# Gating the next loads on q^T, and issuing q^T about a quarter of a unit earlier, in a fused attention and feed-forward kernel

## The chip, the cores and the metric

The kernel runs on one core of one Trainium2 chip. The metric is the device time of one execution in microseconds (us), lower is better. A "span" is the time from the first to the last instruction of the one execution that was profiled, which is 1 to 2 us shorter than its run time.

## The reference

Eight batches of linear attention (Linformer), each with 8 heads, 1024 rows and 64 columns a head; then a feed-forward block on the 8192 x 512 result.

```python
k_proj = np.einsum('ks,bhsd->bhkd', E, k)          # 1024 rows -> 64
v_proj = np.einsum('ks,bhsd->bhkd', F, v)
scores = scale * np.matmul(q, k_proj.transpose(0, 1, 3, 2))
attn = softmax(scores)                             # cut: max, exp, sum
x = np.matmul(attn, v_proj)                        # -> [8192, 512]
h1, h2 = x @ w1, x @ w2
out = np.maximum(h1, h2) @ w_out
```

## The kernel before

All instructions are laid out by hand. The feed-forward block is cut into sixteen units, two for each batch; a unit has down products (`P`, line 636) and, between them, the up products of the next unit (`U`, line 558) in two halves of seven, numbered from 0. The attention of batch b is worked in small steps put into these slots. `("G", n, h)` stands before the up products of half h in unit n; `("U", n, h, i)` after up product i of that half. From batch 3 on one batch needs, in this order:

```python
    for b in range(3, B):
        t = tiles[b]
        n = 2 * b - 3
        at_slot(("G", n, 0), new_attn, t)
        at_slot(("G", n, 0), step_qt_dma, t, 0, H // 2)        # q^T, heads 0-3
        at_slot(("G", n, 0), step_qt_dma, t, H // 2, H)        # q^T, heads 4-7
        at_slot(("U", n, 0, 1), step_kv, t, 0, H, "kv", True, True)  # k, v projected; k turned
        at_slot(("U", n, 0, 6), step_gate, t)                  # waits for the turned k
        at_slot(("U", n, 0, 6), loads, b + 1, "k", "v", "q")   # the next batch's loads
```

The two kinds of transposing DMAs are issued by SyncE, in order with the stores of the output (in batch 4 q^T at 138.16 us, a store at 144.43, the turn of k at 145.46). The gate is a copy of one element on GpSimd; the loads stand behind it in GpSimd's program and were issued after it (in batch 4 the copy ran at 148.30 us, and the k load was issued at 148.81):

```python
    def step_kpt_dma(t):                      # "the turn of k": 512 pieces of 256 bytes
        nc.sync.dma_start_transpose(
            out=t["kpt"], in_=t["kp"].rearrange("p h r d -> p (h r d)"))

    def step_gate(t, n="kpt"):
        nc.gpsimd.tensor_copy(out=junk, in_=t[n][0:1, H - 1, 0:1])

    def load(t, n, src, b, h0, h1):           # float32 in HBM -> float16 on chip, 1024 pieces of 1 KB
        nc.gpsimd.dma_start(
            out=t[n][:, h0:h1],
            in_=src[b, h0:h1].rearrange("h (p c) d -> p h c d", c=NC))
```

The first reader of the turned k is the score product (`score`, line 266), which stands in TensorE's order at `("G", n, 1)`. Batch 2 is turned on TensorE, has no turn of k by DMA, and its gate is on q^T (`step_gate, t, "qt"`).

The softmax here doesn't subtract the row's maximum and nothing guards it: scores larger than these inputs give would overflow.

## Time and profile before

| | before |
|---|---|
| time, median of 3 (range) | 327.46 us (326.99 to 328.31) |
| span of the profiled run | 327.0 us |
| TensorE busy | 317.0 us (97%) |
| granted TensorE clock, mean | 0.998 |

The prediction shows the busy times, the waits and the timelines of one batch and says how to read them. Two more lines: the first, from the page, is the granted clock of TensorE in 40 slices of the span, in tenths of full speed. The second, from the view of the instructions of line 223 (the turn of k), gives the time from issue to landing of its five DMAs: shortest, median, longest.

```profile
PEclk9999999999999999999999999999999999999999
```

```profile
DMA to landing us min/median/max: 2.7/2.7/4.4
```

There is no slice below 9, and the turn of k lands 2.7 us after its issue, but for batch 6 with 4.4.

### The profile page before, as it was taken

To read this page: it belongs to the slowest core of one execution; us is meant where nothing else is said; L and a number is where in the kernel's file an instruction comes from. 1 tells how busy PE (TensorE), PEld (TensorE's weight loads), DVE (VectorE), ACT (ScalarE), POOL (GpSimd) and SP (SyncE) were. 2 spreads that over 40 slices of the span, in tenths; PEclk is the share of its full clock that TensorE was granted. 3 is DMA by queue.
4 is the path that set the end of the run, shared out by engine and by line. 5 is a ranking of instruction groups with operands and counts; after the bars stand their busy time and mean duration, and the time that the engine had idled before them with its cause. 6 is when DMAs were issued, how large, how long until landed. Compare 5 with 4: busy or idle time off the path is not lost.

```text
span 327.0 us, 9015 instructions
## 1 busy us (share of the span) xinstructions
PE 317.0 (97%) x3856; PEld 248.5 (76%) x3856; DVE 239.6 (73%) x424; ACT 201.2 (62%) x359; POOL 37.1 (11%) x56
## 2 busy tenths in 40 slices
PE   8989999999999999999999999998999999999995
PEld 3554446878887788878887888877887888888884
DVE  1345898895969778777967796975967796969572
ACT  2365321667777677667776777656776777765541
POOL 8556002003000120003000300003000000000000
PEclk9999999999999999999999999999999999999999
DMA  8999999988999899996999599886999221312133
GB/s 155 204 199 174 204 207 208 217 187 159 176 239 228 143 146 235 219 186 95 211 220 181 115 188 242 184 163 89 219 209 221 57 97 34 98 34 96 35 116 111
DMA packets 74680, 53.14 MB, mean 163 GB/s; under 512 B 29456, under 2 KB 74512, under 8 KB 74640
## 3 DMA queue, kind: packets, MB, share of 16 engines
q0 software_dynamic: 29376, 28.31, 54.9%
q1 hardware_dynamic: 45264, 24.25, 30.6%
q8 instruction: 30, 0.49, 0.6%
q14 instruction: 10, 0.08, 0.1%
HBM read 57.15 MB, written 16.78 MB: 226 GB/s over the span
## 4 chain that ended last, share of the span: by engine, by line
PE 78%; DMA 17%; DVE 2%; issue 1%; POOL 1%; ACT 0%; SPq 0%; POOLq 0%; DVEq 0%
PE mm_ps L636 44%; PE mm_ps L558 25%; DMA q_sb<-in_q_dram 8%; DMA v_sb<-in_v_dram 4%; PE att_ps L180 3%; PE att_ps L278 3%; PE mm_ps L266 3%; DMA k_sb<-in_k_dram 2%; DMA big<-in_moe_w_dram 2%; DMA kpt_sb<-kp_sb 1%; DVE gt_sb L573 1%; PE mm_ps L237 1%; DVE o_sb L660 1%; DVE xt_sb L381 0%; POOL v_sb L102 0%
## 5 line engine op out<-in xcount | busy, mean ns | idle before, releaser
L529 ACT COPY p_sb<-mm_ps 128x512 f32<-128x512 f32 x172 | 97.2, 593 | 41.3 <-PE mm_ps L558 30.2
L636 PEld LDWEIGHTS <-big 128*128 128x128 f16 x768 | 73.6, 98 | 12.0 <-issue 3.1
L636 PE MATMUL mm_ps<-T_sb,big 128*128 128x256 f16 x576 | 77.8, 273 | 0.0
L573 DVE TENSOR_TENSOR gt_sb<-mm_ps,p_sb 128x512 f16<-128x512 f32 x56 | 38.5, 688 | 47.2 <-PE mm_ps L558 44.0
L558 PE MATMUL mm_ps<-big,big 128*128 128x256 f16 x336 | 50.4, 273 | 0.0
L558 PEld LDWEIGHTS <-big 128*128 128x128 f16 x448 | 43.8, 98 | 5.2
L636 PE MATMUL mm_ps<-wo_sb,gt_sb 128*128 128x256 f16 x256 | 43.0, 273 | 0.1
L636 PEld LDWEIGHTS <-gt_sb 128*128 128x128 f16 x384 | 35.7, 98 | 9.7 <-issue 5.4
L558 PEld LDWEIGHTS <-wd_sb 128*128 128x128 f16 x336 | 32.9, 98 | 3.8
L355 ACT ACTIVATE ex_sb<-mm_ps 128x512 f16<-128x512 f32 x50 | 27.2, 597 | 10.5 <-PE att_ps L278 7.0
L558 PE MATMUL mm_ps<-xt_sb,wd_sb 128*128 128x256 f16 x224 | 33.6, 273 | 0.0
L381 DVE TENSOR_TENSOR xt_sb<-att_ps,ld_sb 128x1024 f16<-128x1024 f32 x26 | 31.7, 1219 | 0.1
L660 DVE TENSOR_TENSOR o_sb<-mm_ps,p_sb 128x512 f32<-128x512 f32 x32 | 21.9, 685 | 7.5 <-PE mm_ps L636 7.5
L636 PE MATMUL mm_ps<-m_sb,xt_sb 128*128 128x256 f16 x128 | 24.4, 273 | 0.0
L608 ACT ACTIVATE gt_sb<-mm_ps 128x512 f16<-128x512 f32 x28 | 16.8, 600 | 10.3 <-PE mm_ps L558 10.3
L519 DVE TENSOR_TENSOR big<-gt_sb 128x1024 f16<-128x1024 f16 x32 | 21.9, 685 | 0.2
L576 DVE TENSOR_SCALAR gt_sb<-gt_sb 128x512 f16<-128x512 f16 (+1 forms) x56 | 20.3, 363 | 1.9
L636 PE MATMUL mm_ps<-T_sb,gt_sb 128*128 128x256 f16 x128 | 21.5, 273 | 0.0
L636 PE MATMUL mm_ps<-wo_sb,big 128*128 128x256 f16 x128 | 21.5, 273 | 0.0
L636 PEld LDWEIGHTS <-xt_sb 128*128 128x128 f16 x192 | 18.8, 98 | 2.2
L229 POOL COPY junk<-kpt_sb 1x1 f16<-1x1 f16 x5 | 1.0, 209 | 162.5 <-DMA kpt_sb<-kp_sb 162.5
L573 DVE TENSOR_TENSOR gt_sb<-p_sb 128x512 f16<-128x512 f32 x28 | 19.1, 681 | 0.0
(85 smaller groups left out, 427.3 us busy)
## 6 DMA issues: line engine op xcount, KB each, us to landing
out_dram<-o_sb SPq DMA_DIRECT2D x63, 256.0 KB, 2.9
k_sb<-in_k_dram POOLq DMA_DIRECT2D x7, 1024.0 KB, 10.6
v_sb<-in_v_dram POOLq DMA_DIRECT2D x7, 1024.0 KB, 18.1
q_sb<-in_q_dram POOLq DMA_DIRECT2D x7, 1024.0 KB, 22.3
k_sb<-in_k_dram POOLq DMA_DIRECT2D x4, 256.0 KB, 7.0
q_sb<-in_q_dram POOLq DMA_DIRECT2D x4, 256.0 KB, 8.1
v_sb<-in_v_dram POOLq DMA_DIRECT2D x2, 512.0 KB, 12.2
big<-in_moe_w_dram POOLq DMA_DIRECT2D x8, 128.0 KB, 9.9
```

Source lines behind the costliest of these rows:

```text
L180: nc.tensor.matmul(out=kv_ps[r * KP : (r + 1) * KP, 0:n], lhsT=eft[:, i, c, :], rhs=t[w][:, h0:h1, c, :], start=(c == 0), stop=(c == NC - 1),)
L266: nc.tensor.matmul(out=banks[e][pos : pos + Z, h * W : (h + 1) * W], lhsT=t["kpt"][o * D : (o + 1) * D, head, s * Z : (s + 1) * Z], rhs=t[ ...
L355: nc.scalar.activation(out=t["ex", g, j][:, e, :], in_=banks[e], func=ACTF.Exp, scale=scale)
L381: nc.vector.tensor_tensor(out=x_out(t, g, j).rearrange("q z o n -> q o z n"), in0=at_ps.rearrange("q o (z n) -> q o z n", z=2), in1=ld[:, ...
L519: nc.vector.tensor_tensor(out=S(i), in0=x, in1=y, op=op)
L529: copy(out=x, in_=bank)
L558: nc.tensor.matmul(out=bank[:, m * W : (m + 1) * W], lhsT=w_[:, n_, (2 * d + m) * 128 : (2 * d + m + 1) * 128], rhs=a[:, n_, :], start=(n ...
L573: nc.vector.tensor_tensor(out=c_blk(j, c), in0=two(x), in1=two(y), op=ALU.add)
L576: nc.vector.tensor_scalar_max(ap, ap, 0.0)
L608: nc.scalar.activation(out=out, in_=in_, func=ACTF.Relu)
L636: nc.tensor.matmul(out=bank[:, i * CH : (i + 1) * CH], lhsT=a(c)[:, i * 128 : (i + 1) * 128], rhs=w_(c), start=(n is not None and m == (lo ...
L660: nc.vector.tensor_tensor(out=o_sb, in0=two(x), in1=two(y), op=ALU.add)
```

## The change

The intent: from batch 4 on q^T is placed earlier, by eight of the 35 groups of matmuls in a unit, and the next loads need no longer wait for the turn of k, so that they too start earlier. Batch 2 gates on the first half of q^T.

```diff
-    def step_gate(t, n="kpt"):
-        nc.gpsimd.tensor_copy(out=junk, in_=t[n][0:1, H - 1, 0:1])
+    def step_gate(t, h=H - 1):
+        nc.gpsimd.tensor_copy(out=junk, in_=t["qt"][0:1, h, 0:1])
 ...
-    at_slot(("U", 1, 0, 6), step_gate, t, "qt")
+    at_slot(("U", 1, 0, 6), step_gate, t, H // 2 - 1)
 ...
-        at_slot(("G", n, 0), new_attn, t)
-        at_slot(("G", n, 0), step_qt_dma, t, 0, H // 2)
-        at_slot(("G", n, 0), step_qt_dma, t, H // 2, H)
+        key = ("G", n, 0) if b == 3 else ("U", n - 1, 1, 3)
+        at_slot(key, new_attn, t)
+        at_slot(key, step_qt_dma, t, 0, H // 2)
+        at_slot(key, step_qt_dma, t, H // 2, H)
```

## The prediction

> **What bounds it.** I read the page first, then one long stretch by engine, then who waited for whom, then the timelines of SyncE and GpSimd around one batch, and last the landings of single transfers.
>
> ```profile
> span 327.0 us, 9015 instructions
> PE 317.0 (97%) x3856; PEld 248.5 (76%) x3856; DVE 239.6 (73%) x424; ACT 201.2 (62%) x359; POOL 37.1 (11%) x56
> PE   8989999999999999999999999998999999999995
> DMA  8999999988999899996999599886999221312133
> ```
>
> TensorE is busy nearly everywhere; the DMA row is full too, but only up to slice 30, after which the kernel is no faster. The table by stretches for 54 to 310 us, the part the change can reach (columns: length, then busy us of PE, PEld, DVE, ACT, POOL):
>
> ```profile
> 54.00:310.00 256.00, 254.57 (x3255) 211.37 (x3256) 198.97 (x354) 175.36 (x321) 14.37 (x21) 1.00 0.83 160
> ```
>
> TensorE is idle for 256.00 - 254.57 = 1.43 us in 256, at full clock. So no rearrangement of DMAs can gain more than about 1.4 us here (0.4%), while a delay that reaches TensorE is paid in full. The waits of TensorE, its weight loads and SyncE's queue (total us, times, longest) name the one transfer concerned:
>
> ```profile
> PE mm_ps L266 <- DMA kpt_sb<-kp_sb: 1.1, 1, 1.1
> ...
> PEld L266 <- DMA kpt_sb<-kp_sb: 1.9, 2, 1.4
> ...
> SPq L249 <- DMA q_sb<-in_q_dram: 7.3, 2, 5.6
> ```
>
> L266 is the score product, which reads the turned k (kpt); 1.1 us of the 1.43 is one wait for it. Around batch 4, SyncE's queue and then GpSimd:
>
> ```profile
> 138.16 6.17 SPq L249 DMA_TRANSPOSE qt_sb<-q_sb  x2
> 144.43 0.53 SPq L651 DMA_DIRECT2D out_dram<-o_sb  x1
> 145.46 1.20 SPq L223 DMA_TRANSPOSE kpt_sb<-kp_sb  x1
> ```
>
> ```profile
> 148.30 0.18 POOL L229 COPY junk<-kpt_sb 1x1 f16<-1x1 f16 x1 [32.01 <-DMA kpt_sb<-kp_sb]
> 148.81 0.88 POOL L102 DMA_DIRECT2D k_sb<-in_k_dram  x1 [0.34 <-PE mm_ps L636]
> ```
>
> The order is q^T (two halves, landing at 143.89 and 145.62 in the trace), one store, the turn of k (landing 148.18), the gate's copy, and only then the loads. So **kpt travels alone**: the loads wait for it. Its landings leave nearly no slack. By landing and the first score weight load: batch 4, 148.18 against 148.59; batch 5, 184.16 against 184.43; batch 7, 256.87 against 257.24. That is 0.3 to 0.4 us each. In batch 3 (113.01) TensorE waited about 0.2 us (weight load 0.49), in batch 6 (221.67, 4.43 us after issue where the others take 2.7) 1.1 us.
>
> [...] while loads and stores run together about 120 load and 115 store packets start per us. [...] So one blocked transfer on SyncE holds all behind it. The trace shows this in batch 3: kpt's input is ready at 109.36, but SyncE is still issuing q^T and one store, and issues kpt at 110.35. [...] instructions arrive in 16 KiB blocks by DMA. The trace has 30 such packets of about 1 us, and those at 140.23, 178.31 and 249.67 each fall with q^T packets that take 1.2 to 2.0 us instead of 0.025; that at 219.69 falls on the end of batch 6's kpt. [...] the late kpt of batch 6 probably stays.
>
> **The change, part by part.** The order of instructions on TensorE, VectorE and ScalarE is the same in both builds; nothing is added. Two things move.
>
> (1) *q^T earlier, batches 4 to 7.* The fourth up product is eight groups of four matmuls ahead of the old place, 8 x 0.44 = 3.5 us, but SyncE is in order: q^T passes one store, not more. It now stands behind the sixth store (136.52 + 0.37 + the short waits = 136.95 in batch 4) and not the seventh (138.16): 1.2 us earlier, likewise 1.1 in batches 5 to 7. [...] its landing moves about 1 us: 144.6, 180.9, 216.9, 253.1. kpt is not issued earlier for that: VectorE ends its input copy at 145.39, 181.24, 217.09, 254.06, and kpt goes out 0.1 to 0.2 us later already. Gain on the path: about 0.
>
> (2) *The gate.* Batches 3 to 6 load on q^T's second half. The v load takes the buffer of the q just turned and waits for q^T anyway. Gate to first load takes 0.5 us (148.30 to 148.81), so loads go out at about 145.2, 181.5, 217.5 instead of 148.81, 184.80, 222.31: 3.3 to 4.8 us earlier, just where kpt goes out (145.46, 181.40, 217.24). TensorE never waits for these loads after 60 us, so arriving earlier is worth nothing, but **kpt loses its empty channel**. How much? A load's first packets come 1.4 us after issue and are sparse: some 3, 19, 16 and 69 in its first four half microseconds, about 100 when full. So they start at 146.6, 182.9 and 218.9. kpt's 512 packets ran from 1.0 to 2.2 us after issue: 146.45 to 147.7, 182.4 to 183.6, 218.3 to 219.5. It meets only the thin front of the loads: 20 to 50 packets against 512, which I estimate at 0.3 to 0.8 us of delay. Less 0.3 to 0.4 us of slack in batches 4 and 5, nothing less in batch 6: 0.2 + 0.3 + 0.5 = about +1.0 us.
>
> (3) *Batch 2* gates on the first half of q^T, so k of batch 3 loads some 2 us earlier; q of batch 3 lands perhaps 1.5 us earlier. SyncE waits 1.64 us for that q at 102.0, so q^T and kpt of batch 3 go out earlier and the wait of about 0.2 us there ends; its loads start about 110.5, first packets near 111.9, as kpt (then issued about 109.5) has finished. Gain 0.2 to 0.5 us.
>
> Sum: +1.0 - 0.4 = +0.6 us on 327.46, **328.0 us**.
>
> **Rivals.** *A: the loads hit kpt fully.* Stores issued into running loads land 7 to 12 us after issue (119.08 to 126.32; 84.75 to 96.95) instead of 2.2. If q^T lands 1 us earlier than I reckon, the loads' full stream is on kpt, which at one load packet per kpt packet needs 512/120 = 4.3 us instead of 1.2: 3 us late, in three batches some 8 us, about 335 us. For it: transposes stall as a whole[...], as the instruction fetches show. Against: the thin front, the in-order stores. *B: a gain.* If kpt of batch 6 was late through q^T and the store queued ahead of it (q^T landed at 217.87, kpt issued 217.24), the earlier q^T frees it: -1.1 us, with batch 3 about 326. Against: the fetch at 219.69. *C: SyncE blocks.* q^T before the seventh store could hold stores if q were late; but q would land before 170 us in batch 5 (172.77 less 3.6), with q^T at 172.8, and four output buffers give room. Then nothing changes: 327.5.
>
> **Range and chances.** The floor is 327.46 - 1.4 = 326.1; the three times before spread over 1.3 us. The tail is upward, from A. I take 326.5 to 331.5. Faster by 2% would need 6.5 us where 1.4 are idle: 0.01. Slower by 2% needs over 2 us of late kpt in each of three batches: 0.11. Within 2%: 0.88.
>
> **What would show it.** Right: loads of batches 5 to 7 issued 3 to 5 us earlier; q^T 1.1 us earlier; kpt issued where it was, landing 3 to 3.5 us after issue in batches 4 to 6 and 2.7 in 7; TensorE's idle time in 54 to 310 us still 1 to 4 us, its waits at L266 on kpt, up. Wrong: kpt landing 5 us or more after issue (A), or at 2.7 in batches 4 to 6 (B); kpt issued earlier; a new wait of SyncE for q; any wait elsewhere than L266.

## The result, and the profile after

The changed kernel takes **340.86 us** (median of 6, 337.37 to 342.09) against 327.48 us (median of 6, 326.73 to 328.92). The ratio is 1.0384, with a 95% interval of 1.0332 to 1.0437: slower, and outside the predicted range. Ratios here are the mean time of one kernel's runs over that of the other's of the same rounds, so not quite the ratio of the medians quoted. From here on "before" in a ratio is the kernel before, run beside the experiment.

The page of the changed kernel, with the rows for busy time and clock:

```profile
span 340.3 us, 9015 instructions
...
PE 321.0 (94%) x3856; PEld 250.0 (73%) x3856; DVE 239.6 (70%) x424; ACT 201.5 (59%) x359; POOL 37.1 (11%) x56
...
PE   7979999999999999959999699996999999999995
...
PEclk9999999999999999987999989999999999999999
```

Three holes appear in TensorE's row (5, 6, 6), and the clock row, all 9 before, dips after the first two. The same stretch of 54 to 310 us, in which TensorE was busy 254.57 us before, and TensorE's waits (total us, times, longest):

```profile
54.00:310.00 256.00, 245.43 (x3135) 201.41 (x3136) 189.42 (x336) 168.29 (x308) 14.33 (x21) 0.98 0.82 156
```

```profile
PE mm_ps L266 <- DMA kpt_sb<-kp_sb: 10.5, 3, 4.2
```

The three holes are one wait, three times: the score products of batches 4, 5 and 6 for the turned k. **The loss adds up from two terms**: this wait grew from 1.3 us (1.1 in batch 6 and 0.2 in batch 3) to 10.5, which is 9.2 us, and TensorE's busy time, for the same 3856 matmuls, grew from 317.0 to 321.0, which is 4.0 us; together 13.2 of the 13.3 us by which the span grew.

Around batch 4 (SyncE, then GpSimd, then the chain of work that ended last: start, length, what):

```profile
145.38 1.20 SPq L223 DMA_TRANSPOSE kpt_sb<-kp_sb  x1
```

```profile
145.00 0.18 POOL L229 COPY junk<-qt_sb 1x1 f16<-1x1 f16 x1 [30.55 <-DMA qt_sb<-q_sb]
145.51 0.88 POOL L102 DMA_DIRECT2D k_sb<-in_k_dram  x1 [0.34 <-issue]
```

```profile
145.38 7.51 DMA kpt_sb<-kp_sb
152.90 0.04 issue
152.94 0.62 PE mm_ps L266 x14
```

The turn of k goes out at 145.38, 0.08 us before its old time, and the load 0.13 us after it. The turn then lands after 7.51 us. In batches 5 and 6 it is 6.42 and 6.69, in batches 3 and 7 it is 2.69:

```profile
DMA to landing us min/median/max: 2.7/6.4/7.5
```

**What the turn waits for** can be seen in the DMA packets in the trace. This is my count, in us from the issue of the turn; its data are 512 packets of 256 bytes, followed by 32 packets of 4 bytes, called completion packets here, as the landing is recorded 0.33 to 1.09 us after the last of them began; the last column counts load packets of 1 KB that began before the middle one of those 32:

```
                    data packets     completion packets       landed   load packets
                    first   last     first  middle  last               ahead
before,  batch 4     1.17   2.22      2.02    2.09   2.25      2.72        0
changed, batch 4     1.18   2.35      4.95    5.70   7.18      7.51      236
changed, batch 5     1.17   2.31      4.09    5.24   5.86      6.42      210
changed, batch 6     1.18   2.29      3.74    4.43   5.60      6.69      172
```

The data go as fast as before. It is the 32 tiny completion packets that start 1.7 to 5 us late, after 172 to 236 load packets. TensorE's score product starts only behind the landing: in batch 4 the last data packet began at 147.73 us, the landing is at 152.89 and the score product at 152.94.

Two limits of this reading. In batches 5 and 6 the first load packet is recorded only 2.91 and 2.60 us after the issue of the turn, later than the last completion packet begins without a load (2.25), and between the last data packet and it no packet of any kind begins. So what holds the completion at first is not a load packet that the trace shows under way. And a part of batch 6 is not the load's: its last completion packet (5.60; the other 31 by 4.90) began just after an instruction fetch of 16 KB that ended at 5.54.

### The profile page after: what moved, and what is told of

Same layout as the page of the kernel before. It is cut to its first block, busy times and chain, and to the rows that moved or that the text cites. A ratio compares the mean times of both kernels' runs of the same rounds, so it can differ in the third digit from the quotient of the medians. Undisturbed runs are those within 1.5% of the kernel's fastest.

```text
span 340.3 us, 9015 instructions
## 1 busy us (share of the span) xinstructions
PE 321.0 (94%) x3856; PEld 250.0 (73%) x3856; DVE 239.6 (70%) x424; ACT 201.5 (59%) x359; POOL 37.1 (11%) x56
## 4 chain that ended last, share of the span: by engine, by line
PE 75%; DMA 21%; DVE 2%; issue 1%; POOL 0%; POOLq 0%; DVEq 0%
PE mm_ps L636 42%; PE mm_ps L558 24%; DMA q_sb<-in_q_dram 8%; DMA kpt_sb<-kp_sb 6%; DMA v_sb<-in_v_dram 4%; PE att_ps L180 3%; PE mm_ps L266 3%; PE att_ps L278 3%; DMA k_sb<-in_k_dram 2%; DMA big<-in_moe_w_dram 2%; DVE gt_sb L573 1%; PE mm_ps L237 1%; DVE xt_sb L381 0%; DVE o_sb L660 0%; POOL v_sb L102 0%
## 5 line engine op out<-in xcount | busy, mean ns | idle before, releaser
L636 PE MATMUL mm_ps<-T_sb,big 128*128 128x256 f16 x576 | 79.4, 277 | 0.0
L558 PEld LDWEIGHTS <-wd_sb 128*128 128x128 f16 x336 | 33.6, 100 | 4.6
L558 PE MATMUL mm_ps<-xt_sb,wd_sb 128*128 128x256 f16 x224 | 35.1, 281 | 0.0
L636 PE MATMUL mm_ps<-wo_sb,big 128*128 128x256 f16 x128 | 22.4, 282 | 0.0
L229 POOL COPY junk<-qt_sb 1x1 f16<-1x1 f16 x6 | 1.1, 176 | 195.7 <-DMA qt_sb<-q_sb 195.7
L266 PE MATMUL mm_ps<-qt_sb,kpt_sb 64*32 64x256 f16 x400 | 10.9, 279 | 10.5 <-DMA kpt_sb<-kp_sb 10.5
```

The costliest lines, as they stand in the source:

```text
L266: nc.tensor.matmul(out=banks[e][pos : pos + Z, h * W : (h + 1) * W], lhsT=t["kpt"][o * D : (o + 1) * D, head, s * Z : (s + 1) * Z], rhs=t[ ...
L558: nc.tensor.matmul(out=bank[:, m * W : (m + 1) * W], lhsT=w_[:, n_, (2 * d + m) * 128 : (2 * d + m + 1) * 128], rhs=a[:, n_, :], start=(n ...
L636: nc.tensor.matmul(out=bank[:, i * CH : (i + 1) * CH], lhsT=a(c)[:, i * 128 : (i + 1) * 128], rhs=w_(c), start=(n is not None and m == (lo ...
```

## The experiments

Theory after the result: a **race**. The completion packets of the turn run 2.0 to 2.3 us after its issue; if a load reaches the engines before that, they stand behind it. A part of the loss is a second effect, the halved clock after a stall (a granted clock of 0.50 from 151.21 to 158.04 us and from 195.58 to 199.00, behind the stalls of batches 4 and 5). Rivals: the early q^T does the harm; the gate's position as such does; or the delay grows smoothly with nearness.

**1. The gate alone.** q^T at its old place, batches 3 to 7 gated on it.

```diff
-        at_slot(("U", n, 0, 6), step_gate, t)
+        at_slot(("U", n, 0, 6), step_gate, t, "qt")
```

> The kernel before with the gate on q^T (second half) in batches 3 to 6 and nothing else; q^T stays at its old place. The loads of the next batch should go out at the landing of q^T + 0.6 us, so about 112.1, 146.2, 182.5 and 218.5, which is 0.8 to 1.7 us AFTER the turn of k is issued, while in the changed kernel they went out 0.1 to 0.5 us after it. Theory (a race): the turn's data is through 2.2 us after its issue and its completion packets directly after, and loads that start later than that do it no harm; then the turn lands after 2.7 to 3.5 us and the time is 327 to 330 us. Rival (loads ahead of the landing of k are bad however late they start): the turn lands after 6 to 7.5 us as in the changed kernel, and the time is 336 to 341 us.

Measured: 327.48 us against 328.6, ratio 0.9981 (0.9943 to 1.002). The loads went out 0.55, 1.26 and 1.41 us after the turns of batches 4 to 6, and those landed after 2.76, 2.77 and 2.71 us. In the stretch of 54 to 310 us TensorE has nearly no idle time left:

```profile
54.00:310.00 256.00, 255.93 (x3264) 212.58 (x3262) 200.49 (x357) 176.14 (x323) 14.36 (x21) 1.00 0.83 159
```

So loads issued before the turn has landed do no harm as such, if they are issued half a microsecond or more after the turn.

**2. The early q^T alone**, the gate on the turned k: the third hunk of the change, and the gate of the kernel before.

> The kernel before with q^T early from batch 4 on and the gate left on the turned k. Theory: q^T lands 1 us earlier, nothing waits for it, the turn of k keeps its empty channel and lands after 2.7 us (batch 6 perhaps 4.4): 327 to 328 us, same. Rival (the early q^T pushes stores into the way of the turn of k, two stores now stand between them): the turn lands 1 us or more later in each batch, 330 us or more.

Measured: 329.03 us against 328.6, ratio 1.0018 (0.9973 to 1.0062). Turns after 2.7 to 2.8 us, batch 6 after 4.22. The early q^T alone does no harm. **Each half of the change is harmless; only together do they lose 13 us**, because the earlier q^T brings the loads 0.4 to 1.0 us nearer to the turn: 0.13, 0.34 and 0.46 us after it, and not 0.55, 1.26 and 1.41.

**3. The changed kernel with the loads held back**: twelve more copies of one element between gate and loads.

```diff
         at_slot(("U", n, 0, 6), step_gate, t)
+        for _ in range(12):
+            at_slot(("U", n, 0, 6), step_gate, t)
         at_slot(("U", n, 0, 6), loads, b + 1, "k", "v", "q")
```

> The changed kernel with 12 more copies of one element between the gate and the loads on GpSimd, in batches 3 to 6: nothing else moves, the loads go out some 1.5 to 2 us later, so 1.3 to 2 us after the turn of k is issued. Theory (a race): the turn lands after 2.7 to 3.5 us in all batches, no half clock, the time returns to 327 to 328.5 us. Rival (the gate on q^T costs in another way, or the loads delay the turn even when they start this late): 333 us or more.

Measured: 328.41 us against 328.6, ratio 1.001 (0.9966 to 1.0054). The copies took longer than expected, the loads came 5.2 to 5.3 us after the turns of batches 4 to 6, and the turns took 2.8 to 3.0 us. The whole loss is undone by time alone.

**4. One copy** in place of twelve. The copies of experiment 3 begin 0.24 us apart, where nothing holds them.

> The changed kernel with ONE more copy of one element between gate and loads (a copy costs about 0.27 us there: twelve moved the loads by some 3.3 us), batches 3 to 6. So far the turn of k landed after 6.4 to 9.9 us wherever the loads were issued up to 0.46 us after it, and after 2.7 to 2.8 us wherever they were issued 0.55 us or more after it. Theory (a cliff between 0.46 and 0.55 us): the offsets become about 0.4, 0.6 and 0.7 us, so at least two of the three turns of batches 4 to 6 land after 2.7 to 3 us; the time falls to 327 to 333 us, most of the 13 us gone for 0.27 us of delay. Rival (delay grows smoothly as the loads come nearer): all three turns land after 5 us or more, time 336 us or more.

Measured: 328.84 us against 327.75, ratio 1.0015 (0.9951 to 1.0079). The offsets became 0.34, 0.55 and 0.53 us, the landings 5.75, 2.70 and 2.77. The one batch that stayed under half a microsecond is the only one that lost, and its stall still cost a stretch at half clock:

```profile
PE mm_ps L266 <- DMA kpt_sb<-kp_sb: 2.4, 1, 2.4
```

**5. The other side of the cliff**: the changed kernel with the gate on the first half of q^T in all batches (`step_gate, t, H // 2 - 1`), so that the k load goes out 1.4 to 3.1 us before the turn.

> The changed kernel with the gate on the FIRST half of q^T in all batches: the k load goes out some 1.5 to 2 us earlier, 1.4 to 2 us before the turn of k, the v load as before. Theory (the completion waits behind load packets already in the engines): no recovery on this side of the cliff; the turn meets a running stream, its data is slowed too, it lands after 7 to 10 us in batches 4 to 6, and batch 3 now suffers as well: 342 to 350 us. Rival (only the cold first packets of a load, which took 0.5 to 2.4 us each, do the harm): the start lies 2 us before the turn's completion, the turn lands after 4 to 5 us, 332 to 336 us.

Measured: 364.44 us against 327.75, ratio 1.1104 (1.1059 to 1.1149), slower than either expectation. Here the data themselves wait: their first packet ran 4.6 to 5.6 us after issue, not 1.2, and the turns landed after 10.2 to 11.3 us in batches 3 to 6. So the cold start of a load is not what harms; a running load is worse.

```profile
PE mm_ps L266 <- DMA kpt_sb<-kp_sb: 29.8, 4, 8.0
```

The turns of batches 3 to 6 in all profiled runs with whole loads (48 turns of 12 kernels), by the offset of the next k load's issue from the turn's issue:

```
offset of the load      turns   landing after issue
-3.21 to -1.02 us          9    9.9 to 11.5 us
-0.08 to +0.46 us          6    5.8 to  7.5 us
+0.53 to +5.54 us         33    2.6 to  3.0 us, but three of them 4.2 to 4.4
```

**A cliff between 0.46 and 0.53 us.** A reckoning fits its place: alone, the first packet of a load ran 1.6 us after its issue, and 0.5 + 1.6 = 2.1, the time at which the completion packets go. It is not shown to be the reason, for in the six turns of the second row the first load packet is recorded 2.1 to 2.9 us after the turn's issue, when the completion packets should have begun. And each kernel has one profiled execution; the four times of experiment 4, 326.69 to 330.40 us, suggest that its turns do not fall the same way each time. The three of 4.2 to 4.4 us each had an instruction fetch of 16 KB beginning 2.06 to 2.45 us after their issue, and their last completion packet began within 5 ns of its end; four other turns with a fetch in these moments were not hurt.

**6. The k load in pieces.** In the changed kernel, four loads of two heads each in place of one of eight; the theory is that the turn lands as late as before, the rival that it lands earlier, as less load is issued at once:

```diff
-                load_all(tiles[b_], b_, n, ...)
+                if n == "k" and b_ >= 4:
+                    alloc(tiles[b_], n)
+                    for h in range(0, H, 2):
+                        load(tiles[b_], n, src, b_, h, h + 2)
```

> The changed kernel with the k load cut into four loads of two heads (256 KB each, same bytes, same order), batches 4 to 7. The first one is issued where the whole one was. Theory (the start of loads is what counts, not how long the DMA is): the turn of k still lands after 6 to 7.5 us, 339 to 343 us. Rival [...]: the turn lands after 3.5 to 5 us, 331 to 336 us.

Measured: 333.04 us against 327.75, ratio 1.0146 (1.0095 to 1.0198); landings 4.21, 4.37 and 5.42 us at offsets of 0.49, 0.23 and 0.35. My theory's number failed and the rival's held in the time and in two of the three landings: how much load is issued at once matters, not only that one has started. The third, 5.42, owes its last part to an instruction fetch: 31 of its completion packets had begun by 3.75 us, the last at 4.44, just after a fetch that ended at 4.38. About 65 to 123 load packets ran before the middle completion packet, where whole loads had 172 to 236.

**7. Cut once more**: one head, then seven. If the amount issued at once matters, the turn should land earlier still.

> The changed kernel with the k load of batches 4 to 7 cut into one head (128 KB[...]) and the other seven heads, issued 0.7 us later. Landing of the turn of k with loads issued 0.1 to 0.5 us after it: 5.8 to 7.5 us with whole loads [...], 4.2 to 5.4 us with loads of two heads [...]. Theory [...]: 3.2 to 4.5 us, time 329 to 333 us. Rival (the cut acted through the later v load, or by chance): 4.5 us or more, 334 us or more.

Measured: 331.11 us against 327.79, ratio 1.0087 (1.0053 to 1.0122); landings 4.34, 3.94 and 5.80 us. The time is as expected, but of the landings only two are, and the offsets differ (0.01, 0.36, 0.60 us; a smaller load also begins earlier after its issue, 1.3 to 1.6 us). In batch 4 the data themselves ran late, 1.99 to 3.47 us after the issue. The 5.80 is again a fetch's doing: 31 completion packets had begun by 3.16 us, the last at 4.66, just after a fetch of 16 KB that ended at 4.59. Without the packets that fetches held, the last completion packet began 4.9 to 7.2 us after the issue with whole loads (six turns), 3.8 to 4.0 with two heads and 3.2 to 3.5 with one. That supports the reading of experiment 6; it doesn't give a law of size.

**8. The clock, first try**: ten matmuls with an unused result before the score products that wait, batches 4 to 6 of the changed kernel. In the trace of the kernel before four matmuls of 128x256 take 0.44 us, so ten of 128x512 are an estimated 2.2 us.

```diff
             banks = [mm_bank(n=2 + e) for e in range(2)]
+            if (g, j) == (0, 0) and any(t is tiles[b] for b in (4, 5, 6)):
+                for m in range(10):
+                    nc.tensor.matmul(out=banks[m % 2], lhsT=ones16[:, 0:128],
+                                     rhs=ones16, start=True, stop=True)
             score(t, g, j, banks)
```

> The changed kernel with 10 matmuls of 128x512 (about 2.2 us at full clock, results overwritten) put in TensorE's order directly before the score products of batches 4 to 6 that wait for the turned k: TensorE works while it would have stood idle. If part of the loss is the granted clock at half after a stall, no stretch at half clock should follow, TensorE's busy time without the fill should go from 321 back to 317 us, and the time should FALL by about 4 us to 336 to 337 in spite of the added work. If the clock has nothing to do with it, the time stays at 340 to 341 (fill hidden in the wait).

Measured: 341.98 us against 328.6, ratio 1.041 (1.0359 to 1.046). The expected fall did not come. The trace says why: no half clock after batches 4 and 5, but in batch 6 the load now got 1.02 us ahead of the turn, which landed after 9.87 us with a half clock behind it. In total it decides nothing, though TensorE's busy time without the fill fell from 321.0 to 318.8 us. The times between the landing of one turn and the issue of the next are of use, within these two runs: with a full clock 32.46 us (changed, batches 6 to 7) and 32.45 and 32.80 (filled, 4 to 5 and 5 to 6); with one window of 3.41 us at half clock 34.11 in both kernels; with two windows 34.87, where in the first TensorE worked only 1.68 us. A window full of work costs about 1.65 us.

**9. The clock, second try**, where the loads are ahead in every batch anyway: experiment 5 with 32 such matmuls before each of its four stalls.

> The kernel with the gate on the first half of q^T (364.4 us; four stalls of 7 to 8 us at the score products of batches 3 to 6, each followed by 3.4 to 7 us of work at half clock, TensorE busy 323.6 us) with 32 matmuls of 128x512 (6.9 us at full clock, results overwritten) directly before each of the four waiting score products. The first fill came out inconclusive in its total, as the loads of batch 6 got ahead of the turn of k; here they are ahead in every batch anyway. If half clock after a stall is part of the loss: no stretch at half clock inside the run, and the time falls by some 6 us, to 357 to 360 us, although 27 us of dummy work are added. If not: 363 to 366 us.

Measured: 358.0 us against 327.79, ratio 1.0913 (1.088 to 1.0947), against 364.44 without the fill (their kernels before gave 327.75 and 327.79). The landings are as late as before (10.0 to 11.5 us), and there is no half clock between the start-up and the end of the run. **Adding 28 us of dummy matmuls made the kernel 6.4 us faster**, and TensorE's busy time without them fell from 323.6 to 318.2 us, so the halved clock is a real part of what a stall costs.

**10. All gates, q^T at the old place.**

> All gates of the change (batch 2 on the first half, the others on q^T) with q^T left at its old place: it should put the loads 0.5 to 1.8 us after the turn of k, on the good side of the cliff, as the gate alone did (span 325.3 us with no wait for the turned k), and batch 3's q^T and turn should go out up to 1 us earlier. Theory: turns after 2.7 to 2.8 us, TensorE idle under 0.5 us in 54 to 310 us, time 326 to 328 us, same as before or up to 0.5% faster. If a turn lands late, its load was issued under 0.5 us after it.

Measured: 328.09 us against 327.75, ratio 1.0006 (0.9959 to 1.0053): same. Turns after 2.7 to 2.8 us, with batch 6 at 4.19 (a fetch).

**11. Batch 2's gate alone.**

> The kernel before with only the gate of batch 2 moved to the first half of q^T. No turn of k by DMA exists in batch 2. The loads of batch 3 start 2 us earlier, q^T and the turn of batch 3 go out up to 1 us earlier, the wait of about 0.2 us for it goes. Theory: 326.5 to 328 us, same. If it is slower by over 2 us, part of the loss of the change lies here and not at the turn of k.

Measured: 326.97 us against 327.79, ratio 0.997 (0.9936 to 1.0004): same. No part of the loss lies here.

**12. A version to keep?** The gate on q^T at the old place, with two more copies for distance from the cliff.

```diff
-        at_slot(("U", n, 0, 6), step_gate, t)
+        for _ in range(3):
+            at_slot(("U", n, 0, 6), step_gate, t, "qt")
```

> A version to keep: the kernel before with the gate on q^T at the old place of q^T, and two more copies of one element before the loads, so that they go out 1.1 us or more after the turn of k in each batch instead of at 0.55 us, at the edge of the cliff. The turn lands after 2.7 to 2.8 us (an instruction fetch may take one to 4.2), TensorE idle 0.1 to 1 us in 54 to 310 us. Time: 0 to 0.4% under the kernel before, 326 to 328 us; not resolvable at 2%.

Measured: 327.14 us against 327.79, ratio 0.9981 (0.9956 to 1.0007). Turns after 2.6 to 2.7 us in all batches, TensorE busy in 255.64 of the 256 us. It is as good as any of them, but no version beats the kernel before beyond the noise; there was 0.4% to be had at most.

## Why the prediction was wrong

- **Where the kernel is bound, and what cannot help**: right. 1.4 us was all there was to gain, and experiments 1 and 12 gained at most about that.
- **The order and the times of the transfers**: right to about 0.3 us in batch 4, but for the order of the last two: the load came 0.13 us after the turn and not 0.26 before it. q^T at 136.97 (predicted 136.95), its second half landed at 144.88 (144.6), the first load at 145.51 (145.2), the turn at 145.38 (145.46).
- **Batch 3**: right in direction. q^T went out at 103.23 instead of 103.67, the turn landed at 112.55 and nobody waited for it.
- **The step that failed** is in part (2): "It meets only the thin front of the loads: 20 to 50 packets against 512, which I estimate at 0.3 to 0.8 us of delay." The turns were delayed by 4.8, 3.7 and 4.0 us against their usual 2.7. The readings under it were a little off (the load's first packet comes 1.6 us after issue and not 1.4, the turn's data begin at 1.17 and not 1.0), and the sum is 328.06 and not 328.0, but none of this makes the difference. I compared amounts of data, as if the two streams shared the engines piece by piece. The data did pass unharmed, as that reckoning says; the completion packets behind them did not, and TensorE waited for the landing after these (7.51 us after issue in batch 4). The term put at +1.0 us measured 9.2 us.
- **A term that was missing**: I treated a stall as costing its own length. Two of the three stalls also halved TensorE's clock, 4.0 us. These are the windows of 3.41 us around the stall of batch 4 (length, TensorE busy, clock, DMA share, GB/s):

```profile
147.79:151.21 3.42, 0.99 (x29) 1.00 0.77 74
151.21:154.62 3.41, 1.68 (x22) 0.50 1.23 199
154.62:158.04 3.42, 3.42 (x18) 0.50 1.25 207
158.04:161.45 3.41, 3.41 (x33) 1.00 1.24 207
```

  A window in which TensorE worked 0.99 us is followed by one at half clock, and that by another. The length of the windows is from the trace: its granted clock changes at 151.21, 158.04, 195.58, 199.00 and 338.94 us, and these lie 2, 11, 1 and 41 times 3.413 us apart.
- **The rival whose sign came true** is A: the turn landed 5 us or more after issue. It got too little weight, 0.11 for slower by over 2%. Its mechanism did not come true: it has q^T land 1 us earlier than reckoned and the turn's data slowed packet by packet, and neither happened. That its 8 us is close to the 9.2 of the wait is luck. Some evidence was in the trace of the kernel before. Stores issued into running loads did not just land late: the one at 119.08 saw its first packet 3.8 us after issue, with some 700 load packets in between, and 0.9 to 1.2 us without loads. That looks like a queue ahead more than a shared rate, and I used it only for the "full stream".
- **Batch 6** of the kernel before: I expected its late turn to stay. It came and went between runs (4.43, 4.22, 4.19, and 2.70 to 2.83 in the others without a load close behind), with fetches at the moment of completion in each late case.

What stays open: what puts the completion packets behind the load. With less load issued at once they were less late: the last one began 4.9 to 7.2 us after the issue with whole loads, 3.8 to 4.0 with two heads and 3.2 to 3.5 with one, leaving out the packets that fetches held. The packets *begin* late (the last at 7.18 in batch 4) and the landing follows as soon after as ever (7.51). The trace shows load packets one by one and does not record the engine, so why the completion is held is not shown, nor is the reason for the pause before the first load packet in batches 5 and 6.

## What to carry to other kernels

A small transfer on the critical path was late here not by the bytes it shared with others, but by the load that was on its way when its completion was to go out: in batch 4 its last data packet began 2.35 us after issue, and it landed at 7.51. Issue bulk loads after it has landed, or at least so late that its completion packets go first (here over half a microsecond after its own issue), and leave a margin, for here one copy of 0.24 us brought back 12 of the 13 us. If a gate looks conservative, ask first what it keeps apart. And look at the granted clock behind each stall of TensorE: here waits of 2.05 us and more were followed by windows at a clock of 0.50, but for two, of 2.42 and 3.31 us.

## What else these traces show

- The nine turns issued into running loads of 1 MB (experiments 5 and 9, and batch 6 of experiment 8) saw their first packet after 4.6 to 5.8 us, with some 390 to 750 load packets in between; without a load it came after 1.17 us. A DMA's completion packets can begin late when its data do not: by 1.7 to 5 us in batches 4 to 6 of the changed kernel.
- Waits of 2.05 us (batch 6 of experiment 6, a window with 1.37 us of matmuls), 2.4 us (batch 4 of experiment 4, 1.34) and 3.06 us (batch 5 of the changed kernel, 1.35) were followed by half clock, and waits of 2.42 us (batch 6 of experiment 7, 1.59 and 2.81 in its two windows) and 3.31 us (batch 6 of the changed kernel, 2.01 and 1.51) were not. So the length of the wait alone did not decide; the matmuls in the windows of 3.41 us did: in these runs, at full clock and after the start-up, up to 1.37 us of them in a window was followed by half clock, and 1.51 or more was not. In the start-up two windows with 2.35 and 3.03 us (experiments 2 and 9) were followed by half clock all the same, so this is no whole rule.
- Instruction fetches of 16 KB (30 in the kernel before, 0.49 MB in all by the page) fell together with held DMA transposes. Around those at 140.23, 178.31 and 249.67 in the kernel before (0.88 to 0.96 us each), no q^T packet at all began for 0.3 to 0.9 us, and some 20 at a time took 1.2 to 2.0 us instead of 0.02. Three of the 33 turns of k that no load disturbed landed after 4.2 to 4.4 us instead of 2.7, with the last completion packet within 5 ns of a fetch's end.
